# Two value heads of every batch loaded through GpSimd's DMA queue instead of SyncE's, in a decode kernel of two interleaved layers

## The chip, the cores and the metric

The kernel runs on one core of one Trainium2 chip. A core has five engines with instruction queues of their own: TensorE (PE, matrix products into PSUM), VectorE (DVE), ScalarE (ACT), GpSimd (POOL) and SyncE (SP), which here only issues DMA transfers. Sixteen DMA engines move data between DRAM and the on-chip memory, SBUF. The metric is the device time of one launch in microseconds; the profile is taken from one execution by the hardware profiler.

## The reference

Eight batch entries, one token each, pass twice through the same pair of blocks, attention (A) and a small feed-forward block (B):

```python
x = x + A(layernorm(x));  x = x + B(layernorm(x))
x = x + A(layernorm(x));  x = x + B(layernorm(x))

def A(x):          # 16 query heads, 8 key/value heads, head size 256
    q = x @ wq
    k, v = k_cache[:, :, 3072:4096], v_cache[:, :, 3072:4096]   # 1,024 keys
    p = softmax((q @ k.T) / 16)
    return (p @ v).reshape(8, 1, 4096) @ wo
def B(x):
    return silu(x @ w1) @ w2      # 448 -> 1792 -> 448
```

All inputs are bf16. For each of 8 batch entries and 8 key/value heads, 512 KB of keys and 512 KB of values are read: 67 MB. Both passes of A use the same keys and values, so each is loaded once and used twice. The weights are some 10 MB.

## The kernel before

**Order of the work.** For each batch entry b (called a batch below), `layer1(b)` transposes the keys on VectorE (L1128, blocks of 32 by 32, in place), computes the scores of the first attention (L791), its softmax and its value products (L859), the output projection (L902) and the sum into the residual. `layer2(b)` runs the feed-forward block (L745, L902), projects the second attention's queries for this batch (L1003 to L1018), and does scores, softmax and value products again from the same keys and values in SBUF. The last feed-forward block is done once for all eight batches in `final()`.

**The ring.** Keys and values go into a ring of 29 slots of 512 KB (one slot: 128 partitions by 2,048 bf16 elements, one head's keys or one head's values). The order of loads is fixed: for each batch the eight heads of keys, then the eight heads of values. Each slot is filled by two transfers of 256 KB (halves h = 0 and 1), so a batch has 32 transfers. A slot is given back by the second attention of the batch that uses it: keys after its scores, values after its value products. A transfer must wait for its slot, and for the transfer issued seven before it to have landed (`AHEAD = 7`).

**Which key is where.** A key's row is 512 bytes. Four neighbouring rows, 2 KB, are one group; a head has 256 groups. In the keys' slot, partition p holds groups 2p (first half) and 2p + 1 (second half); in the values' slot, partition p holds group p (first half) and 128 + p (second). The computation needs the two to match: after the scores are transposed, probability p of a half meets value row p of that half. Any renumbering of groups that is used for both keys and values of a head leaves the result as it is, since softmax and the sum over keys do not depend on their order. `load_k` (L623) and `load_v` (L629) issue the transfers on SP. The values of one half are one contiguous run of 256 KB in DRAM; the keys of one half are 128 rows of 2 KB, 4 KB apart.

**The plan.** No engine's order is written by hand. Every instruction group is a `Task` with an engine, an estimated time and a name; `Plan.schedule` simulates the engines and picks, for each, the next task by rank. SP's tasks keep their program order. A transfer is priced at its bytes over 410 GB/s in one stream (`dma_free`) plus 2 us until it has landed. `best_schedule` runs this once, computes ranks from the tails, adds the table `OFFSETS` (one entry per task name, one table for batches 0 to 6 and one for the last), and schedules again. `emit` then writes each engine's queue in that order, with semaphore waits; an instruction that waits holds up everything behind it on its engine. Where TensorE would be idle, the plan puts in filler products (L1169) that change nothing.

**GpSimd.** Besides setting constants at the start, it computes the second attention's reciprocal root (`rsqrt`, nine small operations at L659 to L675, from the variance that ScalarE writes at L950) and clears a few columns (L1024). The root is used by VectorE at L811 and by ScalarE's exponentials (L817).

## Time and profile before

| | |
|---|---|
| median of 3 runs | 256.47 us (255.53 to 260.47) |
| the profiled execution | 258.16 us |
| its span, first to last instruction | 256.3 us |
| TensorE busy | 198.2 us (77%) |
| VectorE busy | 160.9 us (63%) |
| ScalarE busy | 80.9 us (32%) |
| read from DRAM | 77.67 MB |
| mean granted TensorE clock | 0.993 |

Busy time is summed over the span. An engine's busy share is an average over stages with different limits; what a stage is bound by is read from that stage. In the lists of groups, "out<-in xcount | busy, mean ns | idle before" means the tile written, the tile read, how many instructions, their summed time, the mean of one, and how long the engine sat idle just before them, with what ended it. "DMA share" is the mean busy share of the 16 DMA engines. A DMA issue is the short instruction on the issuing engine; its landing is the moment when the last semaphore increment of the transfer arrives.

### The profile page before, as it was taken

The page shows a single profiled execution, that of the slowest core. Times are in us where ns is not written, and L with a number is a line of the kernel's source. Part 1 is how long each engine was busy: PE and PEld are TensorE (multiplying, and loading weights), DVE is VectorE, ACT ScalarE, POOL GpSimd, SP SyncE. Part 2 cuts the span into 40 slices and gives each one's busy share as a digit, 9 for nine tenths or more (in the row PEclk, how much of TensorE's full clock was granted, in tenths as well). Part 3 has the DMA queues.
Part 4 walks back from the last instruction along what each step waited for, and adds up shares of the span by engine and source line. Part 5 has one row for each costly group of instructions (what it writes and reads, how often), then busy time and mean ns, then how long its engine had stood idle before and what let it go on. Part 6 is the DMA issues. An engine that isn't in the chain of part 4 may idle for free.

```text
span 256.3 us, 8522 instructions
## 1 busy us (share of the span) xinstructions
PE 198.2 (77%) x3595; PEld 97.9 (38%) x3614; DVE 160.9 (63%) x447; ACT 80.9 (32%) x258; POOL 21.5 (8%) x119
## 2 busy tenths in 40 slices
PE   0051686768779788989888998888888989899784
PEld 0051121324344343535343543453344536346441
DVE  7379210087754894798579759965994797444322
ACT  2004320121064306441633254252515440533232
POOL 6100000002000030002001100200020002002000
PEclk9999999799999999999999999999999999999999
DMA  6999999999999989999999899999999999400000
GB/s 236 356 400 402 371 364 391 376 385 386 382 335 387 325 300 296 382 343 323 339 396 348 294 342 372 357 344 353 346 371 328 351 363 379 171 4 3 3 3 1
DMA packets 40341, 78.22 MB, mean 305 GB/s; under 512 B 4320, under 2 KB 6512, under 8 KB 39792
## 3 DMA queue, kind: packets, MB, share of 16 engines
q1 hardware_dynamic: 40304, 77.69, 84.8%
q8 instruction: 28, 0.46, 0.7%
q14 instruction: 9, 0.07, 0.1%
HBM read 77.67 MB, written 0.01 MB: 303 GB/s over the span
## 4 chain that ended last, share of the span: by engine, by line
PE 54%; DVE 20%; DMA 11%; ACT 7%; issue 5%; SPq 2%; DVEq 0%; ACTq 0%
PE bank L859 10%; DMA ring<-in_A_k_cache_dram 9%; PE bank L791 9%; PE bank L902 7%; PE bank L1003 6%; DVE ring L1128 6%; PE bank L1169 6%; DVE qT L1008 3%; PE bank L745 2%; PE bank L1014 2%; DVE qT L754 2%; DVE mseg L799 2%; ACT e_sb L817 2%; DMA ring<-in_A_v_cache_dram 2%; PE bank L823 2%
## 5 line engine op out<-in xcount | busy, mean ns | idle before, releaser
L1128 DVE STREAM_TRANSPOSE ring<-ring 128x512 uint32<-128x512 uint32 x128 | 80.4, 681 | 7.3 <-DMA ring<-in_A_k_cache_dram 7.2
L1169 PE MATMUL bank<-wq_sb,cols_b 128*32 128x512 bf16 (+2 forms) x358 | 41.1, 408 | 2.6 <-issue 2.6
L791 PE MATMUL bank<-ring,qbd 128*16 128x256 bf16 (+2 forms) x808 | 35.1, 317 | 8.3 <-DVE ring L1128 6.8
L859 PE MATMUL bank<-ring,pT_sb 128*4 128x512 bf16 (+1 forms) x512 | 36.0, 378 | 0.4 <-ACT pT_sb L832 0.4
L791 PEld LDWEIGHTS bank<-ring,qbd 128*16 128x16 bf16 (+1 forms) x808 | 20.4, 88 | 20.8 <-DVE ring L1128 9.0
L767 ACT ACTIVATE qbd<-q1s 32x128 bf16<-32x128 bf16 x32 | 10.2, 320 | 50.6 <-PE bank L791 50.0
L1169 PEld LDWEIGHTS bank<-wq_sb,cols_b 128*32 128x32 bf16 (+2 forms) x377 | 12.6, 101 | 18.0 <-issue 13.2
L918 ACT ACTIVATE qT<-bank 128x448 bf16<-128x448 f32 x16 | 8.7, 544 | 34.1 <-PE bank L902 34.1
L1003 PE MATMUL bank<-wq_sb,xn 128*4 128x512 bf16 (+1 forms) x272 | 18.1, 366 | 0.7 <-ACT xn L990 0.4
L840 DVE TENSOR_REDUCE rl_sb<-bank 128x16 f32<-128x128 f32 x16 | 4.5, 284 | 22.3 <-PE bank L836 22.2
L799 DVE TENSOR_REDUCE mseg<-bank 128x1 f32<-128x256 f32 (+1 forms) x24 | 11.8, 493 | 10.3 <-PE bank L791 10.3
L902 PE MATMUL bank<-w2o,oT 128*1 128x448 bf16 x224 | 14.4, 379 | 4.6 <-issue 3.3
L659 POOL TENSOR_SCALAR rstd<-va 128x1 int32<-128x1 int32 x8 | 1.5, 192 | 186.5 <-ACT va L950 186.5
L859 PEld LDWEIGHTS bank<-ring,pT_sb 128*4 128x4 bf16 (+1 forms) x512 | 11.2, 83 | 13.3 <-issue 3.5
L1008 DVE STREAM_TRANSPOSE qT<-bank 128x512 f32<-128x512 f32 (+1 forms) x17 | 11.5, 683 | 5.6 <-PE bank L1003 4.9
L871 DVE TENSOR_TENSOR oT<-bank,rl_sb 128x16 bf16<-128x16 f32 (+1 forms) x32 | 6.3, 197 | 13.6 <-PE bank L866 12.7
L864 ACT ACTIVATE e_sb<-bank 128x512 bf16<-128x512 f32 x16 | 9.6, 597 | 9.2 <-PE bank L859 6.8
L864 ACT ACTIVATE o_sb<-bank 128x512 bf16<-128x512 f32 (+1 forms) x16 | 9.1, 567 | 6.5 <-PE bank L859 6.5
L823 PE MATMUL bank<-ident,e_sb 128*64 128x16 bf16 x128 | 4.9, 184 | 7.2 <-ACT e_sb L817 6.6
L817 ACT ACTIVATE qT<-bank,mb,rstd 128x256 bf16<-128x256 f32 x16 | 8.1, 563 | 6.9 <-DVE mb L813 6.9
L1014 PE MATMUL bank<-qT,irep 128*128 128x64 f32 x32 | 7.5, 324 | 3.4 <-DVE qT L1008 3.4
L946 DVE SCALAR_TENSOR_TENSOR va<-bank,m 128x1 f32<-128x1 f32 x8 | 1.3, 159 | 14.1 <-ACT m L944 12.4
(177 smaller groups left out, 246.0 us busy)
## 6 DMA issues: line engine op xcount, KB each, us to landing
ring<-in_A_k_cache_dram SPq DMA_DIRECT2D x128, 256.0 KB, 5.3
ring<-in_A_v_cache_dram SPq DMA_DIRECT2D x128, 256.0 KB, 4.6
w2o<-in_A_wo_dram SPq DMA_DIRECT2D x2, 1792.0 KB, 11.6
wq_sb<-in_A_wq_dram SPq DMA_DIRECT2D x3, 1024.0 KB, 6.9
w2o<-in_B_w_dram SPq DMA_DIRECT2D x1, 1568.0 KB, 14.9
w_sb<-in_B_w_dram SPq DMA_DIRECT2D x3, 448.0 KB, 12.4
wq_sb<-in_A_wq_dram SPq DMA_DIRECT2D x2, 256.0 KB, 10.0
w_sb<-in_B_w_dram SPq DMA_DIRECT2D x2, 112.0 KB, 11.9
```

The lines of the kernel that those rows point to most:

```text
L767: act(lambda e, q=q: e.activation(qbd[0][32 * q:32 * q + 32].rearrange("p n k (q r) -> p k n q r", r=2)[:, :, :, q, :], q1s[32 * t:32 * t ...
L791: fns.append(lambda e, cb=cb, par=par, j=j, kv=kv, m=m, c0=c0, c1=c1: e.matmul(bank[sc][32 * j:32 * j + m, c0:c1], qbd[layer][:, j * 8 + c ...
L799: dve(lambda e: e.tensor_reduce(mseg[layer][:, ks[0]:ks[-1] + 1], bank[sc][:, lo:hi].rearrange("p (k n) -> p k n", k=len(ks)), AX.X, ALU.m ...
L817: act(lambda e, k2=k2: e.activation(e_sb[ei][:, k2, :, :].rearrange("p uh (jj ul) -> p uh jj ul", ul=2), bank[sc][:, k2 * 256:(k2 + 1) * 2 ...
L859: fns.append(lambda e, qh=qh, uh=uh, j=j, vv=vv: e.matmul(bank[ob][32 * j:32 * j + 2 * w, 0:w * DH], p_col(ei, k2, j, qh, uh, w), vv, star ...
L864: act(lambda e: e.activation(o_sb[oi][:, 0:w * DH], bank[ob][:, 0:w * DH], ACTF.Copy), bk(ob), O_K[oi], 0.2 + w * 0.2, "oevh" if ob == OB[ ...
L902: pe([lambda e, i=i, c=c: e.matmul(bank[XB][32 * c:32 * c + 1, 0:D], rhs(i), w_sb[:, i * D:(i + 1) * D], start=(first and i - i0 < 4), sto ...
L1003: fns.append(lambda e, j=j, c=c, wb=wb, off=off, h0=h0, n=n, k2=k2: e.matmul(bank[wb][32 * j:32 * j + 4, h0:h0 + n], xn[:, part(c, k2), j, :],
L1008: dve(lambda e, wb=wb, h0=h0, n=n: e.transpose(qT[:, h0:h0 + n].rearrange("p (c a i) -> p c a i", a=2, i=32), bank[wb][:, h0:h0 + n].rearr ...
L1014: pe(lambda e, qs=qs: e.matmul(qs.rearrange("p (k c r) -> p k r c", k=4, c=8), irep[:], qT[:].rearrange("p (r c i) -> p i r c", r=2, i=32) ...
L1128: dve(lambda e, v=v: e.transpose(v, v), [("slot", s, h)], [("slot", s, h)], 0.67, "KT")
L1169: fills = {n: [lambda e, j=j, m=P // n: e.matmul(bank[OB[0]][m * j:m * j + m, 0:2 * DH], zero_b.broadcast_to([P, m]), wq_sb[:, 0:2 * DH], ...
```

## The change

In the plan, a GpSimd transfer is a task on GpSimd of 2.0 us (`SWDUR`) whose landing is priced at four times its bytes over 410 GB/s, in a stream of its own (`dma_high`) that doesn't delay SP's. Both tables of `OFFSETS` are replaced, and the second look-ahead goes from 0.25 to 0.15.

```diff
 OFFSETS = (
...
-LOOKS = (0.2, 0.25)
+LOOKS = (0.2, 0.15)
...
+        if dma_key and eng == "pool":
+            t.own, t.land = True, 4 * n_bytes / 410e3 + 3.0
...
+            if best.own:
+                dma_high = max(best.end + 1.0, dma_high) + 4 * best.n_bytes / 410e3
+                best.land = dma_high + dma_lat - best.end
...
-    def dma(fn, writes, n_bytes, key, reads=(), rate=410e3, ahead=None):
-        t = add("sp", fn, reads=reads, writes=writes, n_bytes=n_bytes, dma_key=key, dur=n_bytes / rate, name=key)
+    def dma(fn, writes, n_bytes, key, reads=(), rate=410e3, ahead=None, by_pool=False):
+        if by_pool:
+            t = add("pool", fn, reads=reads, writes=writes, n_bytes=n_bytes, dma_key="p" + key, dur=SWDUR, name="swdge")
+            t.deps[started[-EARLY].idx] = (started[-EARLY], True)
+            return
+        else:
+            t = add("sp", fn, reads=reads, writes=writes, n_bytes=n_bytes, dma_key=key, dur=n_bytes / rate, name=key)
...
+    BY_POOL = {(b, k) for b in range(NB) for k in (0, 2)}
+    SWDUR, EARLY = 2.0, 12
+    turn8, turns = sb("turn8", [8, 8 * len(BY_POOL)], BF16), [0]
+    pool(lambda e: e.inc_swdge_sem([], [], mode="reset_dge_cursor"), [], ["turn8"], 0.1)
+
+    def key_rows(cache, b, kvh):
+        src = cache[b, kvh, S0:SK, :].rearrange("(g x) d -> g (x d)", x=4)
+        return src.rearrange("(l h) n -> h l n" if (b, kvh) in BY_POOL else "(h l) n -> h l n", h=16)
 
     def load_k(s, b, kvh):
-        src = A_k_cache[b, kvh, S0:SK, :].rearrange("(p u) d -> p (u d)", p=P)
+        src = key_rows(A_k_cache, b, kvh)
         for h in range(2):
-            dma(lambda e, h=h: e.dma_start(slots[s][:, 1024 * h:1024 * h + 1024], src[:, 1024 * h:1024 * h + 1024]),
+            dma(lambda e, h=h: e.dma_start(slots[s][:, 1024 * h:1024 * h + 1024], src[:, h:16:2, :]),
                 [("slot", s, h)], W * DH, "slot%d_%d" % (s, h), ahead=AHEAD)
 
     def load_v(s, b, kvh):
-        src = A_v_cache[b, kvh, S0:SK, :].rearrange("(h p u) d -> h p (u d)", h=2, p=P)
+        src = key_rows(A_v_cache, b, kvh)
         for h in range(2):
-            dma(lambda e, h=h: e.dma_start(slots[s][:, 1024 * h:1024 * h + 1024], src[h]),
-                [("slot", s, h)], W * DH, "slot%d_%d" % (s, h), rate=410e3, ahead=AHEAD)
+            dst, part = slots[s][:, 1024 * h:1024 * h + 1024], src[8 * h:8 * h + 8]
+            fns = [lambda e, dst=dst, part=part: e.dma_start(dst, part)]
+            if (b, kvh) in BY_POOL:
+                turns.append(turns[-1] + 4)
+                fns.insert(0, lambda e, c=turns[-1]: e.dma_start(turn8[:, c - 4:c], x2[:, 0:4]))
+            dma(fns, [("slot", s, h)], W * DH, "slot%d_%d" % (s, h), ["turn8"] * (len(fns) - 1), ahead=AHEAD,
+                by_pool=len(fns) > 1)
```

Dependencies that come from the slot (its last readers) are added by `add` for both kinds of transfer.

## The prediction

> **What bounds the kernel now.** I read the slices of the page first, then the DMA queues, then SP's own waits, then windows that run from one batch's first value transfer to the next, and last the chain of waits in the middle of the run.

> ```profile
> span 256.3 us, 8522 instructions
> ...
> DMA  6999999999999989999999899999999999400000
> GB/s 236 356 400 402 371 364 391 376 385 386 382 335 387 325 300 296 382 343 323 339 396 348 294 342 372 357 344 353 346 371 328 351 363 379 171 4 3 3 3 1
> ...
> q1 hardware_dynamic: 40304, 77.69, 84.8%
> ```

> The DMA engines are busy in nine tenths or more of nearly every slice up to the 34th, that is until about 220 us, and all bytes come through one queue. Yet the rate falls from about 400 GB/s in the third and fourth slice to between 294 and 396 later. A busy engine is not always a fast one. (The share can read a little above one; full work here reads 1.02 to 1.05, next block.)

> ```profile
> core 0: us, PE busy (x) PEld busy (x) DVE busy (x) ACT busy (x) POOL busy (x), PEclk, DMA share, GB/s
> 12.80:25.60 12.80, 4.82 (x161) 4.53 (x161) 11.39 (x20) 2.77 (x8) 0.00 (x0) 1.00 1.05 401
> 60.60:84.10 23.50, 19.39 (x382) 9.93 (x389) 15.05 (x39) 7.02 (x20) 0.82 (x5) 1.00 1.02 367
> 84.10:109.60 25.50, 21.68 (x405) 10.36 (x399) 19.47 (x53) 8.97 (x30) 1.93 (x10) 1.00 0.97 328
> 109.60:134.10 24.50, 21.27 (x384) 10.14 (x382) 18.44 (x50) 9.38 (x30) 1.92 (x10) 1.00 0.98 347
> 134.10:158.70 24.60, 21.97 (x395) 10.40 (x394) 19.27 (x54) 9.97 (x31) 1.92 (x10) 1.00 0.97 339
> 158.70:182.60 23.90, 20.72 (x383) 10.46 (x382) 17.55 (x46) 8.89 (x30) 1.93 (x10) 1.00 0.99 349
> 182.60:206.90 24.30, 21.78 (x385) 10.24 (x387) 18.87 (x53) 9.87 (x31) 1.93 (x10) 1.00 1.01 346
> 223.00:256.30 33.30, 26.98 (x534) 14.56 (x535) 11.83 (x49) 10.46 (x36) 2.56 (x13) 1.00 0.01 2
> ```

> The six middle windows are one batch each: their mean is (206.9 - 60.6) / 6 = 24.4 us. A batch loads 32 transfers of 256 KB, 8.39 MB, so 24.4 us is 344 GB/s, which the last column confirms. VectorE works at most 19.5 us of such a window, so no compute engine but TensorE is near full, and TensorE's share holds filler (below). The last window, 33.3 us, has no loads: it is pure computation of the last batch, and whatever moves the last load moves the end by as much.

> ```profile
> SPq L1102 <- ACT ring L1101: 36.8, 1, 36.8
> SPq L623 <- DMA ring<-in_A_k_cache_dram: 18.9, 55, 1.3
> SPq L629 <- DMA ring<-in_A_k_cache_dram: 13.2, 40, 1.2
> SPq L629 <- PE bank L1003: 12.3, 6, 3.0
> ```

> ```profile
> 171.26 6.24 DMA ring<-in_A_k_cache_dram
> 177.53 0.71 DVE ring L1128
> ...
> 194.11 6.55 DMA ring<-in_A_k_cache_dram
> 200.68 1.33 DVE ring L1128 x2
> ```

> SP waits above all for earlier transfers (the rule that at most seven are in flight), in second place, six times for about 2 us, for a ring slot that the computation gives back. The chain of waits goes through key transfers at 171 and 194 us and otherwise from TensorE to VectorE and back. So DMA and computation are closely matched: I read the middle as bound by the DMA stream, with about 1 us a batch lost where a slot came late (a share of 0.97 or 0.98 against 1.02: 4% of 24.4 us).

> **The change part by part.**

> *Four of 32 transfers leave SP.* The other 28 need less of SP:

> ```profile
> L623 SPq DMA_DIRECT2D ring<-in_A_k_cache_dram x128: 327/328/1248, 4.1 to 205.7; - x128
> L629 SPq DMA_DIRECT2D ring<-in_A_v_cache_dram x128: 327/328/1482, 21.1 to 217.4; - x128
> ```

> 32 issues at 0.328 us are 10.5 us of 24.4 on SP, 4 fewer save 1.3 us of an engine that mostly waits: I take 0. [...]

> *The load of the 16 engines.* Now each transfer has 128 rows on both sides, and a batch gives each engine 8.39 MB / 16 = 524 KB. The new value transfers have 8 outer rows on the DRAM side, and the plan in the diff prices them at four times their bytes over the full rate, one after the other in a lane of its own: half of the engines, shared half and half with SP's stream. An 8-row short transfer ahead of each makes the eight always the same eight, if turns are handed out in eights. I take that as what the diff does. Then these eight engines carry 28 x 16.4 + 4 x 32.8 = 590 KB a batch, 1.125 of today, the other eight 459 KB, 0.875. A batch is complete only when all of it has landed, so the fuller half sets the pace. [...]

> What the fuller half needs per batch has two ends. At its present speed when never short of work, 344 GB/s x 1.02 / 0.98 = 358 GB/s or 22.4 GB/s an engine: 590 KB in 26.3 us. At the best window, 401 GB/s or 25.1 GB/s: 23.5 us. The second was reached with little computation and other transfers in it, the first under exactly this load; but the emptier half will leave the memory more room. I take 25.4, two thirds of the way to the slow end. That is +1.0 us a batch, ends -0.9 and +1.9. Seven periods lie between the first and the last batch's values: +7.0 us, ends -6 and +13.

> *GpSimd.* It gets 64 issues, two for each of 32 transfers, and one reset at the start, where nothing waits for it. The trace has no issue from GpSimd. Nearest are SP's 0.33 us (above) and, at the other end, its slowest, 1.48 us: 8 issues a batch are 2.6 to 11.9 us of a 24.4 us batch in which GpSimd works 1.93 us. What stands behind them on GpSimd is the second attention's reciprocal root:

> ```profile
> 115.03 0.19 POOL L659 TENSOR_SCALAR rstd<-va 128x1 int32<-128x1 int32 x1 [19.77 <-ACT va L950]
> ...
> 117.27 0.19 POOL L675 TENSOR_TENSOR rstd<-nt,rstd 128x1 f32<-128x1 f32 x1
> 120.11 0.15 POOL L1024 MEMSET qT<- 128x64 bf16 x1 [2.65 <-PE bank L1014]
> ...
> 123.25 0.23 DVE L811 TENSOR_SCALAR mg<-mg,rstd 128x4 f32<-128x4 f32 x1
> ```

> It ends at 117.46 and is first used at 123.25, 5.8 us later, after 19.8 us in which GpSimd only waited for its input. One pair in front of it, at most 3.0 us, is hidden; a pair that waits there for its slot or for the twelfth SP transfer before it is not, once the wait passes 5.8 us. I take 0 and keep that as a rival.

> *Keys of heads 0 and 2* are read as 16 by 8 rows of the same 2 KB. Bounds are the two patterns that the page has:

> ```profile
> ring<-in_A_k_cache_dram SPq DMA_DIRECT2D x128, 256.0 KB, 5.3
> ring<-in_A_v_cache_dram SPq DMA_DIRECT2D x128, 256.0 KB, 4.6
> ```

> Rows 4 KB apart land in 5.3 us, contiguous ones in 4.6; with several transfers in flight 0.7 us either way is hidden, four times a batch. I take 0, ends -0.1 and +0.4 us a batch (an eighth of 24.4 us times 0.7 / 5.3 is 0.4; a gain that large has no reason).

> *The new order of the computation* (all offsets) removes and adds no instruction. It can gain at most the filler that TensorE runs while it has nothing to do:

> ```profile
> L1169 PE MATMUL bank<-wq_sb,cols_b 128*32 128x512 bf16 (+2 forms) x230 | 27.6, 383 | 1.7 <-issue 1.7
> ```

> (from 60 to 211 us, 4.5 us a batch), and lose as much. Since data sets the pace, I take 0.

> Sum: the profiled execution took 258.16 us, 1.9 over its span of 256.3; the median of three runs is 256.47, close to that span. Span 256.3 + 7.0 = 263.3, and 265.2 with a profile; the median goes by the same step to 263.5, rounded to 263. The ends of load and keys together are 250 (-6.3 - 0.7) and 272 (+13.3 + 2.8); that both terms stand at one end is unlikely, and I take 253 to 269 as the case's own range.

> **The rivals.**

> *The second queue feeds idle engines and the load stays even* (or the turns spread the transfers over all 16). Today the stream dips when SP stands before a slot; GpSimd's transfers stand outside SP's order and fill this. The share then stays at 1.02: 1.0 us a batch, 7 us in all, 249.5 us; with SP's next key transfers also starting earlier, up to 1.5 us a batch, 246. For it: SP's 12.3 us of waits for TensorE. Against it: six waits of 2 us are mostly covered by the seven transfers in flight.

> *Nothing comes of it.* What the half gains in idle moments it pays in load: 256.5, give or take 3. For it: the chain of waits meets few transfers in the middle. Against it: DMA share at or above 0.97 everywhere. [...]

> *GpSimd holds up the root.* A pair ahead of it waits for its slot. SP's waits for slots reach 3.0 us; two in a row and the issues, 3.0, make 9.0, 3.2 over the 5.8 of cover. Over six batches that is +19 us, 275; where only half of the batches meet it, 266. It decides as soon as the wait exceeds 5.8 us. Against it: the order is planned with these waits in it.

> **How the numbers follow.** Uneven load, 263: 0.45. Fed idle engines, 249: 0.30. Nothing, 256.5: 0.18. GpSimd held up, 266 or more: 0.07. Two per cent, about what can be told from no change here (the three runs lie 255.5 to 260.5), is 251.3 and 261.6. Of the first case two thirds lie above 261.6 and a third within; of the second nine tenths are faster. So faster 0.27, within 0.15 + 0.03 + 0.18 = 0.36, slower 0.30 + 0.07 = 0.37. The range runs from inside the second case to the end of the first: 248 to 269, with some 0.1 left out on each side.

> **What would show it.** Uneven load: in the windows of a batch the DMA share falls toward (590 + 459) / (2 x 590) = 0.89 while SP's waits for earlier transfers grow, and periods exceed 25 us. Even load: a share of about 1.0, over 350 GB/s, periods near 23 us, and SP's waits for L1003 shrink. GpSimd held up: VectorE's L811 waits for GpSimd. I am wrong altogether if the loads end well before 220 us, or if the 33 us after them change by more than 2.

## The result, and the profile after

| | before | changed |
|---|---|---|
| median | 258.47 us (4 runs, 255.53 to 260.53) | 300.01 us (4 runs, 295.48 to 304.75) |
| profiled execution, and its span | 258.16, 256.3 us | 295.48, 293.7 us |

The changed kernel takes 1.161 times as long as the one before, with a 95% interval of 1.131 to 1.191. The forecast was 263 us with a range of 248 to 269: the sign was right, and the size lies far outside. A launch can fall into a slower state, so ratios compare the faster runs alone (here 295.48 and 298.91 us against 255.53 and 256.47), and where only one of an experiment's two runs is such a run, it is named first.

First the page of the changed kernel: the span, the slices, the queues and the shares of the chain of waits.

```profile
span 293.7 us, 8433 instructions
...
DMA  6999999999999999989988999999999999910000
GB/s 259 320 348 247 296 340 393 360 263 301 278 376 289 317 311 319 256 255 339 326 239 249 308 317 291 277 313 317 290 261 326 312 336 269 312 40 3 0 2 3
...
q1 hardware_dynamic: 35696, 69.30, 76.4%
q0 software_dynamic: 5632, 8.41, 10.9%
...
DMA 74%; PE 14%; SPq 6%; DVE 3%; ACT 2%; issue 1%; ACTq 0%
```

The same shares of the kernel before:

```profile
PE 54%; DVE 20%; DMA 11%; ACT 7%; issue 5%; SPq 2%; DVEq 0%; ACTq 0%
```

The two lines of slices belong together. The DMA engines are as busy as before, in nine tenths of nearly every slice, but the slices hold 239 to 393 GB/s where before most held 330 to 400. Since the bytes are nearly the same (78.25 and 78.22 MB), the loads end later, at the end of the 35th slice of 7.3 us, near 257 us instead of 220. The chain that ended last is now 74% DMA, where it was 11%.

Windows of the changed kernel, from one batch's first value transfer on SP to the next, three of the six (columns: window, length, busy time and count of PE, PEld, DVE, ACT and POOL, granted clock, DMA share, GB/s):

```profile
70.80:97.50 26.70, 20.57 (x389) 9.83 (x383) 16.19 (x45) 7.50 (x20) 6.64 (x19) 0.94 1.04 317
97.50:127.90 30.40, 22.73 (x412) 10.41 (x407) 21.09 (x56) 10.30 (x35) 8.18 (x22) 1.00 0.98 287
...
212.40:240.20 27.80, 22.02 (x374) 9.89 (x377) 18.43 (x43) 8.78 (x28) 6.11 (x18) 0.94 1.04 307
```

Seven starts, 70.8 to 240.2 us, make six periods of 28.2 us; before they were 24.4. The extra 37.4 us of span are 6 x 3.85 = 23.1 in these periods, 10.2 ahead of them (the first of the seven starts came at 60.6 us before) and 4.1 from the last of them to the end, a stretch that still holds loads. The pure computation at the very end is as long as it was: SP's last wait there is 36.5 us, against 36.8.

Who waits: SP's waits of the changed kernel (total us, times, longest), then VectorE's transposes of the keys, from the list of groups, in the changed kernel and in the one before.

```profile
SPq L1135 <- ACT ring L1134: 36.5, 1, 36.5
SPq L658 <- DMA ring<-in_A_k_cache_dram: 30.8, 29, 2.5
SPq L651 <- DMA ring<-in_A_k_cache_dram: 21.9, 42, 0.9
SPq L658 <- DMA ring<-in_A_v_cache_dram: 18.5, 30, 2.4
```

```profile
L1161 DVE STREAM_TRANSPOSE ring<-ring 128x512 uint32<-128x512 uint32 x128 | 85.9, 696 | 36.6 <-DMA ring<-in_A_k_cache_dram 35.9
```

```profile
L1128 DVE STREAM_TRANSPOSE ring<-ring 128x512 uint32<-128x512 uint32 x128 | 80.4, 681 | 7.3 <-DMA ring<-in_A_k_cache_dram 7.2
```

The transposes themselves cost nearly what they did (696 ns each, 681 before); the idle time ahead of them, waiting for keys, went from 7.3 to 36.6 us. The computation waits for data.

The landing times, from the page:

```profile
ring<-in_A_k_cache_dram SPq DMA_DIRECT2D x128, 256.0 KB, 6.4
ring<-in_A_v_cache_dram SPq DMA_DIRECT2D x96, 256.0 KB, 6.5
ring<-in_A_v_cache_dram POOLq DMA_DIRECT2D x32, 256.0 KB, 9.2
```

Before, keys landed in 5.3 and values in 4.6 us. The second row is the telling one. The rows of those 96 value transfers are untouched by the change, and they too take 6.5 us. A second issuer explains part of that: in two experiments below in which GpSimd issues too, but in plain rows (near ones, and ones 64 KB apart), they land in 5.0 and 4.9 us. The rest suggests that something slows what is in flight beside it.

One window of 8.9 us shows this while TensorE is at rest: 23.4 to 32.3 us, when the first four GpSimd transfers are in flight, beside plain values from SP. Ahead of it, 19.0 to 22.3 us, only plain keys fly.

```profile
19.00:22.30 3.30, 1.19 (x33) 1.03 (x33) 3.20 (x6) 0.31 (x1) 3.21 (x6) 1.00 1.06 399
23.40:32.30 8.90, 0.00 (x0) 0.00 (x0) 4.24 (x7) 1.44 (x4) 0.12 (x1) 1.00 1.07 224
```

399 and then 224 GB/s, both with all 16 engines busy. Half-idle engines, as the prediction had them, would show a lower share. Here the engines work all the time (1.07) and move little. The single packets in the trace say the same. SP's packets of 2 KB, all from plain transfers in these two windows, take 85 ns in the first and 158 in the second. Over the run (mean ns of one packet after the first 15 us; not a view of the page):

```
                            before   changed   64 by 2 and 32 by 4 rows (below)
2 KB packets of SP's queue    91       107        90
4 KB packets of GpSimd's       -       229       173
```

The longer packets are enough to account for the loss. Between the last two columns they differ by 17 ns for 28,672 packets and by 56 ns for 2,048; over 16 engines that is 38 us, and the two spans lie 32 us apart (293.7 and 261.7).

### The profile page after: what moved, and what is told of

It reads as the page before. It is cut to its first block, busy times and chain, and to the rows that moved or that the text cites. A ratio compares the mean times of both kernels' runs of the same rounds, so it can differ in the third digit from the quotient of the medians.

```text
span 293.7 us, 8433 instructions
## 1 busy us (share of the span) xinstructions
PE 200.2 (68%) x3535; PEld 95.4 (32%) x3555; DVE 164.0 (56%) x447; ACT 80.7 (27%) x258; POOL 59.0 (20%) x183
## 2 busy tenths in 40 slices
DMA packets 41366, 78.25 MB, mean 266 GB/s; under 512 B 7392, under 2 KB 9584, under 8 KB 40816
## 4 chain that ended last, share of the span: by engine, by line
DMA 74%; PE 14%; SPq 6%; DVE 3%; ACT 2%; issue 1%; ACTq 0%
DMA ring<-in_A_k_cache_dram 38%; DMA ring<-in_A_v_cache_dram 26%; DMA w2o<-in_B_w_dram 5%; DMA wq_sb<-in_A_wq_dram 4%; PE bank L892 3%; PE bank L935 2%; SPq L614 2%; PE bank L778 1%; SPq L658 1%; SPq L651 1%; PE bank L824 1%; PE bank L1061 1%; PE bank L941 1%; ACT qT L951 1%; SPq L617 1%
## 5 line engine op out<-in xcount | busy, mean ns | idle before, releaser
L1161 DVE STREAM_TRANSPOSE ring<-ring 128x512 uint32<-128x512 uint32 x128 | 85.9, 696 | 36.6 <-DMA ring<-in_A_k_cache_dram 35.9
L824 PE MATMUL bank<-ring,qbd 128*16 128x256 bf16 (+2 forms) x808 | 40.0, 345 | 22.3 <-DVE ring L1161 14.9
L661 POOL DMA_DIRECT2D turn<-in_A_x_dram x32 | 18.4, 574 | 132.8 <-DMA ring<-in_A_k_cache_dram 55.0
L892 PE MATMUL bank<-ring,pT_sb 128*4 128x512 bf16 (+1 forms) x512 | 36.6, 380 | 2.3 <-DMA ring<-in_A_v_cache_dram 1.8
L1202 PE MATMUL bank<-wq_sb,cols_b 128*32 128x512 bf16 (+2 forms) x298 | 31.1, 388 | 1.0 <-issue 0.8
L800 ACT ACTIVATE qbd<-q1s 32x128 bf16<-32x128 bf16 x32 | 10.2, 318 | 58.4 <-PE bank L824 57.8
L832 DVE TENSOR_REDUCE mseg<-bank 128x1 f32<-128x256 f32 (+1 forms) x24 | 12.1, 505 | 23.7 <-PE bank L824 23.6
L658 POOL DMA_DIRECT2D ring<-in_A_v_cache_dram x32 | 21.4, 667 | 0.0
L935 PE MATMUL bank<-w2o,oT 128*1 128x448 bf16 x224 | 15.7, 397 | 6.4 <-DMA w2o<-in_A_wo_dram 5.0
L1036 PE MATMUL bank<-wq_sb,xn 128*4 128x512 bf16 (+1 forms) x272 | 19.2, 388 | 0.9 <-ACT xn L1023 0.4
L873 DVE TENSOR_REDUCE rl_sb<-bank 128x16 f32<-128x128 f32 x16 | 4.5, 281 | 17.7 <-PE bank L869 17.6
L1202 PEld LDWEIGHTS bank<-wq_sb,cols_b 128*32 128x32 bf16 (+2 forms) x318 | 9.9, 96 | 9.7 <-issue 5.6
L935 PE MATMUL bank<-w2o,hT 128*1 128x448 bf16 x106 | 7.5, 368 | 6.5 <-DVE hT L1002 3.9
L1047 PEld LDWEIGHTS bank<-qT,irep 128*128 128x128 f32 x32 | 4.9, 195 | 18.6 <-DVE qT L1041 16.1
## 6 DMA issues: line engine op xcount, KB each, us to landing
ring<-in_A_k_cache_dram SPq DMA_DIRECT2D x128, 256.0 KB, 6.4
ring<-in_A_v_cache_dram SPq DMA_DIRECT2D x96, 256.0 KB, 6.5
ring<-in_A_v_cache_dram POOLq DMA_DIRECT2D x32, 256.0 KB, 9.2
wq_sb<-in_A_wq_dram SPq DMA_DIRECT2D x2, 256.0 KB, 10.3
```

The costliest lines, as they stand in the source:

```text
L658: fns = [lambda e, dst=dst, part=part: e.dma_start(dst, part)]
L661: fns.insert(0, lambda e, c=turns[-1]: e.dma_start(turn8[:, c - 4:c], x2[:, 0:4]))
L824: fns.append(lambda e, cb=cb, par=par, j=j, kv=kv, m=m, c0=c0, c1=c1: e.matmul(bank[sc][32 * j:32 * j + m, c0:c1], qbd[layer][:, j * 8 + c ...
L832: dve(lambda e: e.tensor_reduce(mseg[layer][:, ks[0]:ks[-1] + 1], bank[sc][:, lo:hi].rearrange("p (k n) -> p k n", k=len(ks)), AX.X, ALU.m ...
L892: fns.append(lambda e, qh=qh, uh=uh, j=j, vv=vv: e.matmul(bank[ob][32 * j:32 * j + 2 * w, 0:w * DH], p_col(ei, k2, j, qh, uh, w), vv, star ...
L935: pe([lambda e, i=i, c=c: e.matmul(bank[XB][32 * c:32 * c + 1, 0:D], rhs(i), w_sb[:, i * D:(i + 1) * D], start=(first and i - i0 < 4), sto ...
```

## The experiments

The question of the first group is which part of the change costs; of the second, what in those transfers; of the rest, whether the count of outer rows alone decides, and on which side of the transfer. A transfer is called broken below when its rows in DRAM form two levels with an outer count of 16 or 8 (16 by 8, 8 by 16); plain means 128 rows in one level. The diffs show the lines that matter, long ones cut to the part that differs. A diff is against the changed kernel, the kernel before or an earlier experiment, as said.

**Keys plain again.** The keys of heads 0 and 2 are 128 rows 4 KB apart, as before; all else as in the changed kernel (`key_rows` gets a flag that keeps the plain order). The keys' and the values' numbering of these two heads then no longer match; the work is the same.

```diff
-        src = key_rows(A_k_cache, b, kvh)
+        src = key_rows(A_k_cache, b, kvh, True)
```

> The changed kernel, but the keys of heads 0 and 2 are loaded as 128 plain rows again; their values stay as 8 by 16 rows on GpSimd. Keys and values of these two heads then no longer match, so their part of the attention is another sum; the work is the same. Theory A (a transfer whose DRAM side has two levels of rows slows itself and all that is in flight with it): in the changed kernel the rate was near 270 GB/s while such keys were in flight and near 390 right after, 1.05 MB a batch, 3.9 us against 2.7; taking that away gives back some 1.2 us a batch, so about 10 us of the 300, and the rest stays: 286 to 293 us. Theory B (uneven load of the two halves of the engines): the keys load all 16 engines evenly in either form, so nothing changes: 295 to 303 us.

Measured: 286.95 us (283.45 and 290.44), beside 260.37 for the kernel before. Four key transfers of 32 a batch, of the same bytes and the same 2 KB packets, carried about 14 us (283.45 against 297.2, the mean of 295.48 and 298.91). The prediction had put them at nothing. All of SP's transfers are plain here, and its 2 KB packets still take 99 ns in the mean, against 90 in the experiment with plain rows everywhere.

**No short transfers.**

```diff
-                fns.insert(0, lambda e, c=turns[-1]: e.dma_start(turn8[:, c - 4:c], x2[:, 0:4]))
...
-                by_pool=len(fns) > 1)
+                by_pool=(b, kvh) in BY_POOL)
```

> [...] Theory A (two levels of rows): the rows are as before, 292 to 302 us, and the rate stays near 220 GB/s while GpSimd's transfers are in flight. Theory B (uneven load): the load is even now, most of the loss goes: 250 to 270 us.

Measured: 299.16 us, ratio 1.150 (1.132 to 1.168). The short transfers neither cost nor help in a way that can be told (the rate while GpSimd's first transfers are in flight, 23.4 to 32.3 us, is 264 GB/s, where 220 was expected). Theory B, that uneven load is what costs, expected 250 to 270 us here, and that did not come; that the load is even without the short transfers was its supposition, and no run shows it.

**Plain rows everywhere, GpSimd still issues.** Values of heads 0 and 2 go through GpSimd, with 128 plain rows; no short transfers; the new offsets.

```diff
-        src = key_rows(A_k_cache, b, kvh)
+        src = key_rows(A_k_cache, b, kvh, True)
...
-        src = key_rows(A_v_cache, b, kvh)
+        src = key_rows(A_v_cache, b, kvh, True)
...
-                fns.insert(0, lambda e, c=turns[-1]: e.dma_start(turn8[:, c - 4:c], x2[:, 0:4]))
...
-                by_pool=len(fns) > 1)
+                by_pool=(b, kvh) in BY_POOL)
```

> The changed kernel with keys and values of all heads in plain 128 rows and no short transfers; the values of heads 0 and 2 still come from GpSimd's queue, and the offsets are the new ones. Theory A (two levels of rows): no such transfer is left, so 250 to 262 us, and packets as fast as before. Theory C (a second queue costs by itself, by its descriptors or by taking turns with SP's): a good part of the 40 us stays, 275 us or more.

Measured: 265.31 us, ratio 1.020 (1.005 to 1.034), 3 us above the 250 to 262 that was expected if only the row order costs. Nearly all of the loss is gone with the row order. A second issuer as such is no gain, though, and rather a loss of 2%.

**Offsets alone.** The kernel just shown, with every transfer on SP.

```diff
-                by_pool=(b, kvh) in BY_POOL)
+                by_pool=False)
```

> All transfers by SP in plain rows; only the new offsets, the new look-ahead and the reset of the cursor are left of the change. Theory A: 253 to 264 us. Theory D (the new order of the computation is what costs): 280 us or more.

Measured: 260.03 us, ratio 0.999 (0.990 to 1.009). The new order of the computation by itself is worth nothing either way.

So the row order of the broken transfers is to blame, and three things may matter in it: two levels of rows, the distance between rows, and how the rows are shared out over the 16 engines. The second group takes them apart, with all 128 key transfers at once in the kernel before, so that the effect is large, or with GpSimd's values in the kernels above.

**All keys as 16 runs of 8 neighbouring rows** (rows other than the reference's, of the same bytes, as in the next one).

```diff
-        src = A_k_cache[b, kvh, S0:SK, :].rearrange("(p u) d -> p (u d)", p=P)
+        src = A_k_cache[b, kvh].rearrange("(a y x) d -> a y (x d)", y=16, x=4)
...
-src[:, 1024 * h:1024 * h + 1024]
+src[16 * h:16 * h + 16, 0:8, :]
```

> The kernel before, nothing on GpSimd; the keys of all heads are read as 16 runs of 8 neighbouring rows of 2 KB (16 KB in one piece, then 16 KB skipped), so the DRAM side has two levels of rows but lies nearly in one piece. They are other rows of the same head than the reference wants; the work is the same. [...] Theory R (rows 32 or 64 KB apart in DRAM are slow to read): no such rows here, 255 to 264 us.

Measured: 279.73 us, ratio 1.085 (1.063 to 1.106), 3 us under the 283 to 297 that the author put if all keys load at the 270 GB/s seen with such keys in the changed kernel, and far above the 255 to 264 of theory R. Slow without any far rows, and without GpSimd.

**All keys as 128 plain rows 64 KB apart.**

```diff
+        src = A_k_cache.rearrange("b k s d -> (b k s d)").rearrange("(r n) -> r n", n=32768)
+        i0, c0 = 256 * kvh, 1024 * b
...
-src[:, 1024 * h:1024 * h + 1024]
+src[i0 + P * h:i0 + P * h + P, c0:c0 + 1024]
```

> The kernel before, nothing on GpSimd; the keys of all heads are read as 128 plain rows of 2 KB that lie 64 KB apart in the key cache, the distance that the changed kernel has within a run. They are other rows than the reference wants; the work is the same. Theory M (placement on the SBUF side): plain rows, so 255 to 264 us. Theory R (far rows): 283 us or more, with a rate near 270 GB/s while keys are in flight.

Measured: 256.50 us, ratio 0.993 (0.989 to 0.998). Distance in DRAM costs nothing here, on SP's queue.

**GpSimd's values as 16 by 8 rows** in place of 8 by 16, with plain keys and no short transfers, so that all 16 engines can take part (the share reads 1.02 in the window below).

```diff
-src[8 * h:8 * h + 8]
+src[:, 8 * h:8 * h + 8] if (b, kvh) in BY_POOL else src[8 * h:8 * h + 8]
```

> The kernel of e1 (plain keys, new offsets, values of heads 0 and 2 on GpSimd) without short transfers, and with the values' DRAM side as 16 by 8 rows instead of 8 by 16, so that all 16 engines can share one transfer. Values then don't match their keys for these heads; the work is the same. [...] Theory H (what costs is that eight engines carry the whole transfer): 262 to 268 us, as with plain rows.

Measured: 284.35 us, ratio 1.102 (1.083 to 1.122), against 283.45 and 290.44 with 8 by 16 (and short transfers). A number of rows that 16 engines can share evenly doesn't save it. That speaks against the uneven load as the main cost.

**GpSimd's values as 128 plain rows 64 KB apart** (others than the reference's).

```diff
+            if (b, kvh) in BY_POOL:
+                far = A_v_cache.rearrange("b k s d -> (b k s d)").rearrange("(r n) -> r n", n=32768)
+                part = far[256 * kvh + P * h:256 * kvh + P * h + P, 1024 * b:1024 * b + 1024]
```

> The kernel of e3 (plain rows for all, values of heads 0 and 2 on GpSimd without short transfers), but those values are read as 128 plain rows that lie 64 KB apart in the value cache; other rows than the reference wants, the work is the same. Theory M and theory H: 262 to 268 us, as e3. Theory R: 275 us or more.

Measured: 269.17 us, ratio 1.044 (1.028 to 1.059), where the same kernel with near rows had 1.020 (1.005 to 1.034): 3.9 us more by the two medians, a little above the 262 to 268 that was expected, and far from the 284 to 300 of the broken orders. The two intervals just meet, so whether far rows cost something on GpSimd's queue stays open.

What remained was the outer count. The third group varies it.

**The changed kernel with outer counts of 64 and 32**: keys 64 by 2, values on GpSimd 32 by 4 rows; short transfers, issuer and offsets as changed.

```diff
-"(l h) n -> h l n" if (b, kvh) in BY_POOL else "(h l) n -> h l n", h=16)
+"(l h) n -> h l n" if (b, kvh) in BY_POOL else "(h l) n -> h l n", h=64)
...
-src[:, h:16:2, :]
+src[:, h:4:2, :]
...
-src[8 * h:8 * h + 8]
+src[32 * h:32 * h + 32]
```

> The changed kernel with one size changed: the DRAM side's outer count is 64 in place of 16 for the keys of heads 0 and 2 (64 by 2 rows) and 32 for their values on GpSimd (32 by 4 rows in place of 8 by 16); the short transfers, GpSimd's share and the new offsets stay. [...] If a DRAM side of two levels costs as such, whatever its count: 285 us or more. [...]

Measured: 263.74 us, ratio 1.022 (1.013 to 1.031). This is the experiment that counts most: everything that the change does is still there, two levels of rows included, and 33 to 36 us are gone (297.2 or the median 300.01 against 263.74). The time lies within the 258 to 272 us that the author put if outer counts of 8 and 16 are what costs. What stays, 2%, is what GpSimd's issue costs with plain rows too.

**All keys as 32 runs of 4 neighbouring rows**, the partner of the 16 by 8 rows above (the diffs of this one and the next two are against it).

```diff
-src[16 * h:16 * h + 16, 0:8, :]
+src[32 * h:32 * h + 32, 0:4, :]
```

> The kernel before with all keys as 32 runs of 4 neighbouring rows (other rows than the reference's, of the same bytes). [...] If two levels of rows cost as such: about 280 us, as 16 by 8 rows did.

Measured: 260.01 us, ratio 0.998 (0.990 to 1.007), within the 254 to 264 that the author put if an outer count of 32 costs nothing; 16 by 8 rows took 279.73.

**All keys as 8 runs of 16 neighbouring rows.**

```diff
-"(a y x) d -> a y (x d)", y=16, x=4)
+"(a y x) d -> a y (x d)", y=32, x=4)
...
-src[16 * h:16 * h + 16, 0:8, :]
+src[8 * h:8 * h + 8, 0:16, :]
```

> The kernel before with all keys, issued by SyncE, as 8 runs of 16 neighbouring rows (other rows than the reference's, of the same bytes). If such a transfer keeps to 8 of the 16 engines, these carry 16 x 32 KB + 16 x 16 KB = 768 KB a batch in place of 512 KB, and the load alone makes the streaming half as long again: 315 to 380 us, with the DMA share well under 1. If the uneven load matters little beside the placement: 275 to 295 us, near the 280 us of the 16 by 8 rows.

Measured: 330.66 us, ratio 1.282 (1.270 to 1.293). This is the uneven load that the prediction spoke of, on SP and for every key, and it reads quite differently, as the windows below show. The packets of 4 bytes fit it. The kernel before has 4,320 of them on SP's queue, 16 for each transfer, and so have the kernels with 32 by 4 and 16 by 8 keys; this one has 3,296, eight fewer for each of the 128 key transfers, as if eight engines took part.

**All keys as 16 by 8 rows, DRAM order turned round**: the outer count of 16 steps by one row of 2 KB and the inner count of 8 by sixteen rows, so that each transfer reads 256 KB in one piece. The SBUF side of the transfer is not edited.

```diff
-"(a y x) d -> a y (x d)", y=16, x=4)
+"(y a x) d -> a y (x d)", a=16, x=4)
...
-src[16 * h:16 * h + 16, 0:8, :]
+src[:, 8 * h:8 * h + 8, :]
```

> [...] If the cost lies in where the engines write in SBUF: 270 to 290 us. If it lies in the 16 separate runs of DRAM that the engines read: 254 to 262 us.

Measured: 280.33 us (276.44 and 284.23), beside 258.85 for the kernel before. By 276.44 the loss is 17.6 us, where the other 16 by 8 order lost 21.0 (279.73 against 258.75). So most of the loss is there in either DRAM order.

The same window, 18 to 24 us, of five kernels, in which only key transfers fly. The last two columns are DMA share and GB/s. Before (128 plain rows):

```profile
18.00:24.00 6.00, 1.27 (x33) 1.03 (x33) 5.97 (x10) 2.77 (x8) 0.00 (x0) 1.00 1.05 402
```

32 by 4:

```profile
18.00:24.00 6.00, 1.27 (x33) 1.03 (x33) 5.93 (x10) 2.77 (x8) 0.00 (x0) 1.00 1.05 392
```

16 by 8, the order of the first of these experiments (16 runs of 8 neighbouring rows):

```profile
18.00:24.00 6.00, 1.27 (x33) 1.04 (x33) 5.29 (x10) 1.78 (x6) 0.00 (x0) 1.00 1.06 279
```

16 by 8, DRAM order turned round:

```profile
18.00:24.00 6.00, 1.27 (x33) 1.03 (x33) 5.57 (x10) 2.01 (x6) 0.00 (x0) 1.00 1.06 297
```

8 by 16:

```profile
18.00:24.00 6.00, 0.23 (x1) 0.10 (x1) 3.49 (x8) 0.00 (x0) 0.00 (x0) 1.00 0.53 200
```

Divide the rate by the busy engines (share x 16). Before: 402 / 16.8 = 23.9 GB/s for a busy engine. With 32 by 4: 23.3. With 16 by 8: 279 / 17.0 = 16.5, and 17.5 in the turned order. With 8 by 16: 200 / 8.5 = 23.6. There are two illnesses. On SP's queue an outer count of 8 leaves the engines idle for about half of their time (share 0.53), and while busy they run at full speed (23.6 GB/s): the share shows it. An outer count of 16 keeps all of them busy (1.06), and each moves some 30% less (16.5 GB/s): the share hides it, and only the rate tells.

The window of the first GpSimd transfers, 23.4 to 32.3 us (the changed kernel's stands above), in four kernels. GpSimd's values as 8 by 16, keys plain:

```profile
23.40:32.30 8.90, 0.79 (x8) 0.26 (x12) 3.27 (x5) 0.00 (x0) 0.00 (x0) 1.00 1.06 254
```

As 16 by 8:

```profile
23.40:32.30 8.90, 1.77 (x20) 0.62 (x24) 3.32 (x5) 0.00 (x0) 0.00 (x0) 1.00 1.02 329
```

All plain:

```profile
23.40:32.30 8.90, 3.59 (x32) 0.97 (x32) 3.63 (x6) 0.45 (x3) 0.00 (x0) 1.00 1.03 394
```

Counts of 64 and 32, all else as changed:

```profile
23.40:32.30 8.90, 3.59 (x32) 0.94 (x32) 3.63 (x6) 0.36 (x1) 0.00 (x0) 1.00 1.05 405
```

254, 329, 394 and 405 GB/s at nearly the same share: GpSimd's broken transfers have the second illness, and the 8 by 16 form among SP's plain transfers doesn't leave engines idle here (share 1.06). With 16 by 8 the first four transfers are over sooner (their last 4 KB packet starts at 27.4 us, against 30.9), and still that kernel takes as long as the 8 by 16 one. Over the run its packets are nearly as slow (220 ns for 4 KB and 97 for 2 KB; 236 and 99 with 8 by 16; 178 and 90 with plain rows). The 8 by 16 transfers may load the engines unevenly all the same: each leaves 64 packets of 8 bytes beside its 64 of 4 KB, and the other forms leave none. That this means eight engines for the data is the author's guess, and what it adds is not shown.

**The old order of the computation with GpSimd's transfers**: the plain-rows kernel with the `OFFSETS` and `LOOKS` of before. This asks about the 2% that remain.

```diff
-LOOKS = (0.2, 0.15)
+LOOKS = (0.2, 0.25)
```

(and both tables of `OFFSETS` as before)

> Plain rows everywhere, the values of heads 0 and 2 issued by GpSimd, no short transfers, with the old offsets and look-ahead. If the 2% of the same kernel with the new offsets came from the order in which slots come free: 254 to 260 us. If it comes from GpSimd's issue itself: 262 to 268 us.

Measured: 273.97 us, ratio 1.066 (1.056 to 1.075); both expectations missed. The new offsets, worth nothing while SP issues all, are worth 8.7 us by the two medians once GpSimd issues (ratios 1.066 and 1.020). SP's waits and one window of this kernel show how the old order fails:

```profile
SPq L659 <- PE bank L1036: 22.2, 3, 11.8
```

```profile
117.00:120.00 3.00, 2.30 (x42) 1.13 (x42) 1.12 (x5) 1.07 (x5) 0.00 (x0) 1.00 0.42 156
120.00:125.00 5.00, 4.31 (x89) 2.21 (x85) 2.27 (x6) 3.11 (x13) 1.75 (x9) 1.00 0.00 0
```

SP stands up to 11.8 us before a slot that the computation gives back late (its value transfers wait for earlier transfers and for slots alone, and the profile names a TensorE line), and the DMA engines run empty for 5 us. With the new offsets such holes are smaller but there. The plain-rows kernel of the first group, SP's waits for slots and its two thinnest windows:

```profile
SPq L651 <- PE bank L891: 16.8, 10, 4.4
...
SPq L658 <- PE bank L823: 10.7, 3, 5.0
```

```profile
84.00:108.00 24.00, 21.18 (x381) 10.04 (x377) 17.51 (x46) 7.99 (x28) 1.90 (x10) 0.93 0.85 305
...
204.00:228.00 24.00, 19.38 (x349) 9.73 (x350) 15.94 (x42) 5.98 (x22) 4.09 (x14) 0.93 0.81 294
```

Here the share falls (0.85, 0.81) and with it the rate: engines without work, because slots came late. That the 2% come from this and from nothing else fits these rows, but no run isolated it. No version with GpSimd's transfers was as fast as the kernel before.

## Why the prediction was wrong

The account of the 41.5 us, by medians: plain keys instead of 16 by 8 give back 13.1 (300.01 to 286.95); values of 32 by 4 instead of 8 by 16 on GpSimd some 23.2 more (286.95 to 263.74; that kernel's keys are 64 by 2); 4.9 remain over the 258.80 of the kernel before beside it. With 297.2 and 283.45 in place of the first two medians the steps are 13.7 and 19.7. The kernels before of the groups, on several chips, differ by up to 2 us, and the two runs with plain keys by 7, so the split between keys and values is good to some 4 us.

*The step that failed* is the cost of the row order, in both places. For the keys the prediction wrote "I take 0, ends -0.1 and +0.4 us a batch". It took as bounds the landing of contiguous and of 4 KB-strided rows, both 128 plain rows, and so compared distances in DRAM. The kernel with rows 64 KB apart shows that distance is worth under 1%; what is new in these transfers, two levels of rows with an outer count of 16, was in neither row. Measured: 13 to 14 us, 1.6 to 1.7 us a batch over eight. For GpSimd's values it asked how many bytes each engine carries, +1.0 us a batch for a fuller half that works on at today's speed beside a half that idles. With all keys as 8 by 16 rows on SP a half of the engines' time is idle (share 0.53); that eight engines carry GpSimd's 8 by 16 rows as well, and always the same eight, was the author's supposition, and no run shows it. The changed kernel's windows show no half without work (0.96 to 1.04 for all 16); they show all engines slow, and 2.5 to 2.9 us a batch (19.7 to 23.2 over eight), nearly alike whether the rows come as 8 by 16 or as 16 by 8. The sign of the forecast was therefore luck: it came from a fuller half that sets the pace.

*A smaller miss* is the move of the issues itself. The terms for SP, GpSimd and the new order were all 0; with plain rows the move costs 2%, some 5 us (265.31 against 260.37).

*Its signatures* gave the verdict. "Uneven load: the DMA share falls toward 0.89": it read 0.96 to 1.04 in the six windows from 70.8 to 240.2 us. "Even load: a share of about 1.0, over 350 GB/s": the share is there and the rate isn't. The case that came, a full share at 287 to 317 GB/s, was not on the list, because the prediction took a busy engine's speed as given, though its own first paragraph says that a busy engine is not always a fast one. SP's waits for earlier transfers did grow, as said, but they would under any slower stream.

*The uneven load is real* where it applies: with all keys as 8 by 16 rows on SP the share falls to 0.53 and the time to 330.66 us. An estimate of the prediction's kind holds there: if eight engines carry all keys and a half of the values, each has 786 KB a batch, at the 23.6 GB/s measured in this kernel 33 us, 9 more than 24.4, and 8 x 9 = 72 over 258.8 is 331. That it meets the microsecond is chance; with seven periods, as the prediction counted, it would give 322.

*Right steps.* No run shows a gain from SP's saved issues. The new order alone is worth nothing (0.999), though it isn't once GpSimd issues: a term taken by itself missed that it goes with another. GpSimd holds up no compute engine: a pair of its issues takes 0.57 + 0.67 = 1.24 us, inside the cover of 5.8 us,

```profile
L658 POOL DMA_DIRECT2D ring<-in_A_v_cache_dram x32: 637/671/705, 19.3 to 241.6; - x32
```

(the value issues of the changed kernel: ns, shortest, median and longest), and no wait of VectorE, ScalarE or TensorE for GpSimd shows. The computation after the loads did not change.

*The rival that GpSimd feeds idle engines*, 0.30, fell: with plain rows its transfers take the time to 1.020, not below one.

*The mechanism.* Shown with all keys on SP: an outer count of 16 on the DRAM side slows each busy engine from 23.9 to 16.5 GB/s, and 32 doesn't (23.3). With 64 by 2 keys and 32 by 4 values in the changed kernel the loss is gone too (263.74 us). The other DRAM order leaves most of it (17.5 GB/s). Plain transfers in flight beside broken ones slow down with them (85 to 158 ns a packet). Why an outer count of 16 slows the engines was not shown. The author's guess, by elimination, is where in SBUF they write: no trace tells which partitions an engine writes, and no run changed these alone.

One thing speaks for caution. The 8 by 16 rows on SP showed no such loss in the engines that were busy: 23.6 GB/s each, and beside plain values 93 ns for a 2 KB packet over the run, against 91 before. Why the same form is slow on GpSimd's queue (236 ns for 4 KB, against 178 with plain rows) stays open; no run settled it.

## What to carry to other kernels

Look at the DMA share and the GB/s as a pair: here share down meant engines without work (0.81 and 0.85 with late slots, 0.53 with an outer count of 8), and share full with the rate down meant engines that are busy and slow (1.06 and 279 GB/s with an outer count of 16, where plain rows gave 1.05 and 402), and then plain transfers beside them suffered as well (85 to 158 ns a packet). For a 128-partition load of 2 KB rows like these keep 128 rows in one level, or an outer count of 32 or 64 where two levels are needed (32 for all keys took 0.998 of the time before, 64 and 32 in the changed kernel 1.022); 16 and 8 cost 8% and 28% here when all keys had them. And look at the packets' own durations: they told plain from broken (85 and 158 ns) where the share didn't (1.06 and 1.07). And when a queue is split, give the plan an order made for it, or the waits for slots cost as they did here (1.066 with the old order, 1.020 with the new).

## What the runs showed of the hardware that was not expected

- On SP's queue the distance of the rows hardly matters: with all keys as 128 rows of 2 KB, 64 KB apart, the kernel took 0.993 (0.989 to 0.998) of the time with rows 4 KB apart.
- GpSimd's transfers move in packets of 4 KB where SP's move the same rows in packets of 2 KB: in the kernel with counts of 64 and 32, 173 ns for 4 KB and 90 ns for 2 KB, so about the same rate (23.7 and 22.7 GB/s).
- Packets of SP's plain transfers lengthen when broken ones fly beside them: 99 ns for 2 KB where only GpSimd's values are broken, 90 where all rows are plain. The 4-byte packets of SP's queue lengthen as well, from 9.1 to 10.1 ns.
- Short transfers ahead of GpSimd's made no difference that can be told (299.16 and 300.01 us), at 0.57 us of GpSimd each.
